# Splitting one sigmoid in two on ScalarE so that GpSimd's half of a gate comes first

**Chip, cores, metric.** One core of one Trainium2 chip. The time is device microseconds of one launch.

## The reference

```python
def _attn_ref(x):                       # x: (8, 3136, 256) fp32
    X = np.fft.fft(x, axis=1)
    X = np.fft.fft(X, axis=2)
    return X.real.astype(np.float32)

def _moe_ref(x, w_in, conv_w, w_out):   # d_ff = 1024, 3 taps
    h = np.maximum(x @ w_in, 0.0)
    # conv_out: depthwise convolution of h over the sequence, 3 taps
    gate = 1.0 / (1.0 + np.exp(-conv_out))
    return (h * gate @ w_out).astype(np.float32)
```

## The kernel before

The main loop has 256 steps: 8 batches, 4 chunks of positions, 8 slices of 128 rows of d_ff. A chunk is 769, 770, 770 or 833 columns wide. A step goes through these functions at different times; the loop is a software pipeline. In the same steps, side work prepares the next batch: VectorE folds x and builds w, TensorE does a part of the Fourier transform (`pd`), ScalarE copies half of its result (`as`), VectorE finishes it into `pt` and `qt`, and GpSimd treats one single row (`er`).

```python
    def combine(s):        # VectorE, one input in PSUM (a), one in SBUF (c): h
        ...
    def first_tap(s):      # ScalarE: g = h * cw[0]
        ...
    def other_taps(s):     # VectorE, h and g both in SBUF: "the taps", L504
        for k in (1, 2):
            stt(out=g, in0=h[:, k:k + n], scalar=cw[:, k, f:f + 1], in1=g, op0=ALU.mult, op1=ALU.add)

    def sigmoid(s):
        act(gs[s], gs[s], AF.Sigmoid)

    def gate(s):
        ...
        m = n // 2
        gt(g[:, m:n], g[:, m:n], h[:, m + 1:n + 1], op=ALU.mult)   # GpSimd, upper half
        vt(g[:, 0:m], g[:, 0:m], h[:, 1:m + 1], op=ALU.mult)       # VectorE, lower half

    # ---- where the side work of batch b is placed
        for i, u in enumerate(us):
            ...
            at(cs[i + 1], "act", u.copy)
            if i == 4:
                at(cs[i + 1], "dve", row)      # DMA er <- qt
            at(cs[i + 1], "dve", u.fin)        # for i == 4: GpSimd's work on er

    for t in range(n + LAG):
        ...
        if 0 <= t - 2 < n:
            sigmoid(steps[t - 2])
        if t + 1 < n:
            products(steps[t + 1])             # TensorE: pb, pa
            copies(steps[t + 1])               # ScalarE: nb <- pb, L481
        run("act")
        if t < n:
            combine(steps[t])
        run("load")
        run("dve")
        if t + 2 < n:
            seed(steps[t + 2])
        if t < n:
            first_tap(steps[t])
        if 0 <= t - 1 < n:
            other_taps(steps[t - 1])
        if 0 <= t - 2 < n:
            gate(steps[t - 2])
        if t >= LAG:
            mm2(steps[t - LAG])                # TensorE: po, needs both halves of g
        run("pe")
```

Each engine's list has this order, and its instructions in the timelines follow it: on ScalarE of the kernel before L507 starts at 631.33, L481 at 632.47, L309 at 633.23, L466 (`seed`) at 634.10 and L498 at 634.62.

## Time and profile before

| kernel before | |
|---|---|
| time, median of 4 runs | 1309.3 us (1307.4 to 1310.5) |
| span of the profiled run | 1303.7 us |
| TensorE / VectorE / ScalarE / GpSimd busy | 1203.4 / 1190.7 / 857.4 / 406.7 us |
| TensorE's wait for VectorE's half of the gate | 22.0 us in 43 waits |
| TensorE's wait for GpSimd's half of the gate | 14.9 us in 9 waits |

The busy shares cannot say which of two nearly full engines sets the time. The waits of TensorE for the gate can: they are the stretches in which VectorE or GpSimd is ahead of it in the chain. The prediction shows these lines.

### The profile page before, as it was taken

The numbers are of one execution on the slowest core, as the hardware profiler recorded it, in microseconds if no ns is written. First come the engines' busy times: TensorE is split into PE (matmuls) and PEld (weight loads), VectorE is DVE, ScalarE is ACT, GpSimd is POOL, SyncE is SP. The second block draws the span as 40 slices with busy tenths as digits, with TensorE's granted clock in tenths as the row PEclk, the third lists the DMA queues.
The fourth block names the chain that finished last, engine by engine and source line by source line (L and its number), as shares of the span: only waits on it lengthen the run. The fifth ranks groups of instructions, "written<-read, shape, count | busy, mean of one in ns | idle before, by whom it ended". The sixth has DMA issues, their size and how long they took to land.

```text
span 1303.7 us, 15202 instructions
## 1 busy us (share of the span) xinstructions
PE 1203.4 (92%) x4914; PEld 898.9 (69%) x4914; DVE 1190.7 (91%) x1664; ACT 857.4 (66%) x1558; POOL 406.7 (31%) x507
## 2 busy tenths in 40 slices
PE   0758999999999999999899999999999999999998
PEld 0525677777677766777677776777677777777776
DVE  6869999999999998999899998999989888898996
ACT  0226676666667666677667776766767777777885
POOL 2415434241523234232513225241322223122222
PEclk9968999999999999999999999999999999999999
DMA  7601203020211112020202103020010001000011
GB/s 227 185 25 45 80 25 99 1 77 25 88 36 49 49 29 74 25 77 25 72 29 62 39 25 94 30 76 1 25 50 25 27 25 42 20 14 27 25 33 43
DMA packets 46841, 66.02 MB, mean 51 GB/s; under 512 B 5601, under 2 KB 35197, under 8 KB 46505
## 3 DMA queue, kind: packets, MB, share of 16 engines
q1 hardware_dynamic: 41012, 49.80, 12.1%
q0 software_dynamic: 5120, 12.85, 3.4%
q10 hardware_dynamic: 628, 2.40, 0.6%
q8 instruction: 38, 0.62, 0.2%
q14 instruction: 43, 0.34, 0.1%
HBM read 39.24 MB, written 25.74 MB: 50 GB/s over the span
## 4 chain that ended last, share of the span: by engine, by line
PE 57%; DVE 26%; issue 8%; ACT 4%; POOL 2%; DMA 2%; DVEq 0%; POOLq 0%; ACTq 0%; SPq 0%
PE po L89 36%; PE pb L89 8%; DVE g L504 7%; PE pa L89 7%; PE pd L89 6%; DVE h L492 4%; DVE g L515 4%; ACT nb L481 2%; DVE w L174 2%; DVE w L175 1%; DVE xh L158 1%; DVE xh L147 1%; DVE xh L163 1%; POOL er L319 1%; DVE xh L162 1%
## 5 line engine op out<-in xcount | busy, mean ns | idle before, releaser
L89 PE MATMUL po<-wout,g 128*128 128x256 f32 (+2 forms) x3200 | 744.9, 383 | 37.4 <-DVE g L515 22.0
L89 PEld LDWEIGHTS po<-wout,g 128*128 128x128 f32 (+2 forms) x3200 | 598.6, 189 | 206.0 <-DVE g L515 59.2
L504 DVE SCALAR_TENSOR_TENSOR g<-h,cw,g 128x770 f32<-128x770 f32 (+2 forms) x512 | 579.9, 1133 | 10.9 <-ACT g L498 1.8
L514 POOL TENSOR_TENSOR g<-g,h 128x385 f32<-128x385 f32 (+1 forms) x256 | 240.5, 941 | 775.4 <-ACT g L507 434.7
L507 ACT ACTIVATE g<-g 128x770 f32<-128x770 f32 (+2 forms) x256 | 220.6, 862 | 253.3 <-DVE g L504 252.2
L481 ACT ACTIVATE nb<-pb 128x386 f32<-128x386 f32 (+4 forms) x512 | 225.8, 494 | 95.7 <-PE pb L89 94.0
L492 DVE CUSTOM_DVE_ANT_0 h<-pa,nb 128x386 f32<-128x386 f32 (+4 forms) x512 | 265.1, 559 | 14.6 <-PE pa L89 9.6
L498 ACT ACTIVATE g<-h,cw 128x770 f32<-128x770 f32 (+2 forms) x256 | 243.8, 952 | 0.7 <-DVE h L492 0.7
L89 PE MATMUL pa<-pt,G 128*128 128x386 f32 (+2 forms) x512 | 213.6, 498 | 9.1 <-ACT pa L466 9.1
L89 PE MATMUL pb<-qt,G 127*128 127x386 f32 (+2 forms) x512 | 215.7, 502 | 4.5 <-ACT nb L481 4.5
L466 ACT ACTIVATE pa<-eb,ge 128x386 f32<-128x386 f32 (+2 forms) x256 | 154.0, 602 | 8.1 <-DMA eb<-ed 8.1
L515 DVE TENSOR_TENSOR g<-g,h 128x385 f32<-128x385 f32 (+2 forms) x256 | 153.0, 598 | 4.2 <-ACT g L507 4.2
L89 PEld LDWEIGHTS pa<-pt,G 128*128 128x128 f32 x512 | 97.5, 191 | 83.6 <-issue 21.0
L89 PE MATMUL pd<-tab,w 99*128 99x196 f32 (+2 forms) x448 | 119.0, 375 | 0.0
L89 PEld LDWEIGHTS pb<-qt,G 127*128 127x128 f32 x512 | 94.3, 191 | 31.8 <-ACT nb L481 7.7
L122 POOL DMA_INDIRECT xh<-in_x_dram,idx x64 | 88.8, 1388 | 16.4 <-issue 12.8
L89 PEld LDWEIGHTS pd<-tab,w 99*128 99x128 f32 (+1 forms) x448 | 83.7, 191 | 13.7
L531 ACT COPY os<-po 128x256 f32<-128x256 f32 (+2 forms) x200 | 59.8, 393 | 17.1 <-DMA out_dram<-os 9.6
L158 DVE TENSOR_TENSOR xh<-xh 98x1024 f32<-98x1024 f32 (+1 forms) x32 | 46.6, 1460 | 0.1
L147 DVE TENSOR_TENSOR xh<-xh 98x1020 f32<-98x1020 f32 (+1 forms) x32 | 45.6, 1435 | 0.0
L89 PE MATMUL po<-win,dm 128*128 128x512 f32 x8 | 5.7, 879 | 38.4 <-DMA dm<-dft_dim_dram 38.4
L174 DVE TENSOR_TENSOR w<-xh 98x508 f32<-98x508 f32 (+1 forms) x32 | 31.1, 971 | 0.1
(84 smaller groups left out, 350.8 us busy)
## 6 DMA issues: line engine op xcount, KB each, us to landing
out_dram<-os SPq DMA_DIRECT2D x184, 128.0 KB
xh<-in_x_dram SPq DMA_DIRECT2D x16, 784.0 KB
eb<-ed SPq DMA_DIRECT2D x16, 193.0 KB
tab<-dft_seq_dram SPq DMA_DIRECT2D x4, 601.8 KB
raw<-in_moe_w_in_dram ACTq DMA_DIRECT2D x2, 1024.0 KB
raw<-in_moe_w_out_dram SPq DMA_DIRECT2D x1, 2048.0 KB
eb<-ed SPq DMA_DIRECT2D x8, 209.0 KB
eb<-ed SPq DMA_DIRECT2D x8, 192.5 KB
```

The source lines that it names most:

```text
L89: nc.tensor.matmul(o, l, r, start=start, stop=stop, skip_group_check=True)
L122: nc.gpsimd.indirect_dma_start(out=xh[b, h][0:NP, 4 + m].rearrange("p q d -> p (q d)"), out_offset=None, in_=bass.AP(tensor=x.tensor, offs ...
L158: vt(flat(to, to + 2), flat(0, 2), flat(2, 4), op=op)
L466: act(pa[s][:, 0:n], eb[b, c], AF.Copy, scale=ge[:, f:f + 1])
L481: act(nb[s][:, i, cols], p[:, cols], AF.Copy, scale=-1.0 if i else 1.0)
L492: nc.vector._custom_dve(TENSOR_ADD_SAT, out=to, in0=a[:, cols], in1=c[:, i, cols], s0=BIG, s1=0.0)
L498: act(gs[s], hs[s][:, 0:n], AF.Copy, scale=cw[:, 0, s[2]:s[2] + 1])
L504: stt(out=g, in0=h[:, k:k + n], scalar=cw[:, k, f:f + 1], in1=g, op0=ALU.mult, op1=ALU.add)
L507: act(gs[s], gs[s], AF.Sigmoid)
L514: gt(g[:, m:n], g[:, m:n], h[:, m + 1:n + 1], op=ALU.mult)
L515: vt(g[:, 0:m], g[:, 0:m], h[:, 1:m + 1], op=ALU.mult)
L531: nc.scalar.copy(out=osb[0:m, j % 2], in_=pt[0:m, j % 2])
```

## The change

GpSimd multiplies the upper half of the gate. With one sigmoid for the whole width it waits until the lower half is done too: 0.92 us from the sigmoid's start, 271.08 to 272.00 in the timeline that the prediction shows. The change does the upper half first, so that GpSimd starts earlier.

```diff
     def sigmoid(s):
-        act(gs[s], gs[s], AF.Sigmoid)
+
+        n = gs[s].shape[1]
+        for c in (slice(n // 2, n), slice(0, n // 2)):
+            act(gs[s][:, c], gs[s][:, c], AF.Sigmoid)
```

Line numbers after it shift by 3: GpSimd's half is L514 before and L517 after, VectorE's L515 and L518, the sigmoid L507 and L510.

## The prediction

> **What bounds the kernel now.** I read the page first (busy shares and groups), then the waits of TensorE, then the timeline of one steady batch step by step. "Step" is one pass of the main loop: one 128-row slice of F for one chunk of positions. There are 256, in 8 batches of 32.
>
> ```profile
> PE 1203.4 (92%) x4914; PEld 898.9 (69%) x4914; DVE 1190.7 (91%) x1664; ACT 857.4 (66%) x1558; POOL 406.7 (31%) x507
> ```
>
> TensorE and VectorE are both near full, ScalarE and GpSimd are not. The windows of the single batches say the same: batches 0 to 5 take 152 to 155 us with VectorE 143 to 148 us busy and TensorE 147 to 149; batch 6 takes 145 with TensorE busy 144; batch 7 takes 125 with TensorE busy 124. So the last two batches are TensorE's alone, and in the first six the two engines hand the lead to each other. The groups that matter:
>
> ```profile
> L504 DVE SCALAR_TENSOR_TENSOR g<-h,cw,g 128x770 f32<-128x770 f32 (+2 forms) x512 | 579.9, 1133 | 10.9 <-ACT g L498 1.8
> L514 POOL TENSOR_TENSOR g<-g,h 128x385 f32<-128x385 f32 (+1 forms) x256 | 240.5, 941 | 775.4 <-ACT g L507 434.7
> L507 ACT ACTIVATE g<-g 128x770 f32<-128x770 f32 (+2 forms) x256 | 220.6, 862 | 253.3 <-DVE g L504 252.2
> L515 DVE TENSOR_TENSOR g<-g,h 128x385 f32<-128x385 f32 (+2 forms) x256 | 153.0, 598 | 4.2 <-ACT g L507 4.2
> ```
>
> GpSimd's 775 us of idle is its own and costs nothing by itself; what matters is when its multiply (L514) runs. The timeline of two steps of batch 1 shows that:
>
> ```profile
> 271.08 0.85 ACT L507 ACTIVATE g<-g 128x769 f32<-128x769 f32 x1 [2.02 <-DVE g L504]
> 271.43 1.02 DVE L492 CUSTOM_DVE_ANT_0 h<-pa,nb 128x385 f32<-128x385 f32 x2
> 271.56 2.86 PE L89 MATMUL po<-wout,g 128*128 128x256 f32 x12 [0.72 <-DVE g L515]
> 272.00 0.86 POOL L514 TENSOR_TENSOR g<-g,h 128x385 f32<-128x385 f32 x1 [4.05 <-DVE h L492]
> 272.36 2.38 DVE L504 SCALAR_TENSOR_TENSOR g<-h,cw,g 128x769 f32<-128x769 f32 x2
> ...
> 274.77 0.85 ACT L507 ACTIVATE g<-g 128x769 f32<-128x769 f32 x1 [0.76 <-DVE g L504]
> 275.12 1.02 DVE L492 CUSTOM_DVE_ANT_0 h<-pa,nb 128x385 f32<-128x385 f32 x2
> 275.69 0.86 POOL L514 TENSOR_TENSOR g<-g,h 128x385 f32<-128x385 f32 x1 [1.80 <-DVE h L492]
> 276.05 1.05 DVE L174 TENSOR_TENSOR w<-xh 99x508 f32<-99x508 f32 x1
> 277.02 0.68 DVE L175 TENSOR_TENSOR w<-xh 99x508 f32<-99x508 f32 x1
> 277.62 2.07 DVE L504 SCALAR_TENSOR_TENSOR g<-h,cw,g 128x769 f32<-128x769 f32 x2
> ...
> 280.21 2.86 PE L89 MATMUL po<-wout,g 128*128 128x256 f32 x12 [0.59 <-DVE g L515]
> ```
>
> The sigmoid starts when VectorE's taps (L504) end; 0.92 us later GpSimd starts its 0.86 us multiply. VectorE is meanwhile in the combine (L492, one input in PSUM), which runs at its usual 1.02 us for two. The instruction after the combine has two SBUF inputs, and it is stretched for as long as GpSimd still runs: the taps take 2.38 us in the first step and 2.07 in the second, where GpSimd is done before they start; there L174 takes 1.05 us instead of about 0.68. The stretch is GpSimd's end (272.86) less the combine's (about 272.45): 0.3 to 0.4 us. Steps with 833 columns show 0.39 to 0.42. Taking each form's tenth-percentile duration in the trace as undisturbed, the stretch sums to about 55 us on L504, 10 on L515 and 29 on the folding operations: some 94 us of VectorE's busy time.
>
> [...]
>
> **The change part by part.** Nothing moves between engines, and no queue is reordered; ScalarE's list gains 256 instructions.
> 1. *ScalarE.* 256 sigmoids of 862 ns become 512 of half the width. [...] ScalarE has 102 to 106 us busy in a batch of 152 to 155, so this mostly fills idle time.
> 2. *GpSimd.* The half that it multiplies comes first, so its start moves from 0.92 us after the sigmoid's start to about 0.60, an estimate: 0.32 us earlier (0.35 with 833 columns). The duration is as before.
> 3. *VectorE.* GpSimd now ends about 0.05 us after the combine instead of 0.37. Each stretched pair loses about 0.32 us. GpSimd's new start is still after L515, so it does not collide there. I find about 150 steps of 256 where GpSimd starts straight after the sigmoid and an operation with two SBUF inputs follows, so L504 should lose some 35 to 45 us of its 580 and the folds about 12.
> 4. *What of it reaches the end.* Only where TensorE waits for VectorE. Those waits are few:
>
> ```profile
> PE po L89 <- DVE g L515: 22.0, 43, 1.9
> PE po L89 <- POOL g L514: 14.9, 9, 2.9
> ```
>
> By batch the first is 8.7, 4.0, 3.0, 2.3, 2.0, 2.0, 0 and 0 us. The gap in the issue of matmuls is some 0.16 us larger each time, so about 29 us, the upper limit. But not all these waits come from a stretched chain. Many follow a step like this one:
>
> ```profile
> 314.20 0.52 DVE L258 TENSOR_TENSOR qt<-as,pd 128x197 f32<-128x197 f32 x1 [1.33 <-ACT as L254]
> ...
> 316.06 2.06 DVE L504 SCALAR_TENSOR_TENSOR g<-h,cw,g 128x770 f32<-128x770 f32 x2
> ...
> 318.64 2.86 PE L89 MATMUL po<-wout,g 128*128 128x256 f32 x12 [0.36 <-DVE g L515]
> ```
>
> VectorE first waited 1.33 us for TensorE's transform (pd, through ScalarE), then ran unstretched (2.06 us, GpSimd was long done), and TensorE waited for the result. Nothing in that loop gets shorter. I went through the waits one by one and allowed each only the stretch that lies between VectorE's last idle time (or the previous wait) and it, 0.32 us a step and never more than the gap. Batch 0: steps 1 to 10, each with a fold, run without a break, 10 x 0.32 = 3.2 us, and two later waits 0.7: 4. Batch 1: 2.6. Batch 2: 1.0. Batches 3, 4 and 5: three waits each of about 0.33, 0.29 and 0.5, so 1.1 each. Batches 6 and 7: nothing. The sum is about 11 us.
> 5. *Taken back.* In a few steps the copies behind the sigmoid (L481, then the transform's copy L254) start the moment it ends, and VectorE waits for them; there 0.1 us is lost, some two steps a batch, under 2 us in all.
>
> 1308.8 - 11 + 1.5 = **1299 us**, 0.7% faster.
>
> **The rivals.**
> *The saving on VectorE goes all the way.* If VectorE paced the first six batches throughout, about 0.32 us x 20 steps x 6 = 38 us would come off: 1270 us, 3% faster. For it: VectorE hardly pauses in most steps, and the chain of the page gives it 26%. Against it: TensorE's own matmuls issue in about 144.6 us a batch, so that most of the 153 us is already TensorE, and after a saving VectorE would only wait longer for pd.
> *ScalarE becomes the bound or delays the chain.* It would lose 0.1 to 0.2 us a step where its copies release VectorE: up to 0.15 x 200 = 30 us, 1335. For it: L481 follows the sigmoid in order, and L254 follows L481. Against it: ScalarE waits 94 us in all for TensorE's pb just before L481, and 252 us for L504 before the sigmoid; both swallow the extra.
> *GpSimd is late for another reason.* Nine waits on its multiply (14.9 us) stand behind the single-row work on er (L317 to L319, up to 2.4 us each) and not behind the sigmoid; likewise where its indirect transfers are in the way. Then the earlier half changes nothing: if this held more widely, the time stays at 1305 to 1309.
>
> **Range and chances.** The step accounting can err by half on either side: 4 to 17 us saved, and a little more if shorter VectorE steps let TensorE run ahead over several steps; on the other side the full ScalarE cost. I take 1288 to 1308. Two per cent faster would need 26 us, almost all the waits, 5%; two per cent slower needs a new bound, 2%.
>
> **What the profile after would show.** Right: a sigmoid half of 0.51 to 0.55 us; GpSimd's multiply starting about 0.6 us after the first half's start; L504's mean down from 1133 to about 1050 ns; VectorE's busy time down 40 to 60 us while the span falls far less; TensorE's wait for VectorE's gate down from 22 us to 12 to 15, left mostly behind transform steps; VectorE's waits for as (L254, L273) longer. Wrong: L504 unchanged (then GpSimd doesn't start earlier, or collides elsewhere); VectorE's gate waiting for the second half; L481 waiting no longer for pb; or the span falling by as much as VectorE's busy time.

## The result, and the profile after

1289.3 us, median of 4 runs (1287.4 to 1290.5): a ratio of 0.9847, 95% interval 0.9829 to 0.9865, or 20 us off. A ratio here is the mean time of one kernel's fast runs over that of the other's of the same rounds, so not quite the ratio of the medians quoted. The predicted 1299 us had half of this gain; the time lies 1.3 us inside the lower end of the predicted range.

The page of the changed kernel, busy shares and groups:

```profile
PE 1198.0 (93%) x4914; PEld 898.6 (70%) x4914; DVE 1153.2 (90%) x1664; ACT 880.2 (68%) x1814; POOL 404.1 (31%) x507
L504 DVE SCALAR_TENSOR_TENSOR g<-h,cw,g 128x770 f32<-128x770 f32 (+2 forms) x512 | 556.9, 1088 | 11.0 <-ACT g L498 1.5
L510 ACT ACTIVATE g<-g 128x385 f32<-128x385 f32 (+3 forms) x512 | 244.1, 527 | 187.6 <-DVE g L504 187.3
```

VectorE is 37.5 us less busy. The taps' mean fell from 1133 to 1088 ns. A half sigmoid takes 527 ns.

The timeline of the changed kernel at the two steps that the prediction showed:

```profile
269.25 0.94 ACT L510 ACTIVATE g<-g 128x385 f32<-128x385 f32 x2 [1.46 <-DVE g L504]
269.60 1.02 DVE L492 CUSTOM_DVE_ANT_0 h<-pa,nb 128x385 f32<-128x385 f32 x2
269.74 2.86 PE L89 MATMUL po<-wout,g 128*128 128x256 f32 x12 [0.22 <-DVE g L518]
269.86 0.86 POOL L517 TENSOR_TENSOR g<-g,h 128x385 f32<-128x385 f32 x1 [3.13 <-ACT g L510]
270.53 2.07 DVE L504 SCALAR_TENSOR_TENSOR g<-h,cw,g 128x769 f32<-128x769 f32 x2
...
273.92 0.72 DVE L174 TENSOR_TENSOR w<-xh 99x508 f32<-99x508 f32 x1
```

GpSimd starts 0.61 us after the sigmoid's start (0.92 before). The taps take 2.07 us (2.38 before) and L174 0.72 us (1.05 before). TensorE's wait at the start of the first step has gone from 0.72 to 0.22 us.

The waits of TensorE after:

```profile
PE po L89 <- DVE g L518: 13.7, 27, 1.6
PE po L89 <- POOL g L517: 12.7, 10, 2.1
```

To see where the time came from I took every pair of successive matmuls in both traces and subtracted the first one's own time at full clock (the median distance of starts for its shape, 215 ns for 128x256 and 326 ns for 128x386) from the distance of their starts. What is left is a gap. Summed over the steps of a batch:

| batch | 0 | 1 | 2 | 3 | 4 | 5 | 6 | 7 | all |
|---|---|---|---|---|---|---|---|---|---|
| gaps before, us | 17.6 | 9.6 | 9.9 | 8.4 | 9.2 | 8.5 | 2.1 | 1.4 | |
| gaps after, us | 13.7 | 6.7 | 7.6 | 6.0 | 6.0 | 4.7 | 2.1 | 1.5 | |
| less by | 3.9 | 2.9 | 2.3 | 2.4 | 3.2 | 3.8 | 0 | -0.1 | 18.4 |
| predicted | 4 | 2.6 | 1.0 | 1.1 | 1.1 | 1.1 | 0 | 0 | 11 |

Batches 0 and 1 came as predicted. Batches 2 to 5 gave 11.7 us where 4.3 were predicted. Step by step, 5.0 of these 11.7 us lie at the waits for GpSimd's gate that stand behind its work on `er`. The prediction had said that nothing changes there. The other 6.7 us lie at waits for VectorE.

### The profile page after: what moved, and what is told of

It is laid out like the page before. It is cut to its first block, busy times and chain, and to the rows that moved or that the text cites. A ratio compares the mean times of both kernels' runs of the same rounds, so it can differ in the third digit from the quotient of the medians.

```text
span 1288.0 us, 15443 instructions
## 1 busy us (share of the span) xinstructions
PE 1198.0 (93%) x4914; PEld 898.6 (70%) x4914; DVE 1153.2 (90%) x1664; ACT 880.2 (68%) x1814; POOL 404.1 (31%) x507
## 4 chain that ended last, share of the span: by engine, by line
PE 69%; DVE 17%; issue 4%; ACT 4%; DMA 3%; POOL 2%; DVEq 0%; SPq 0%; ACTq 0%; POOLq 0%
PE po L89 43%; PE pb L89 10%; PE pa L89 9%; PE pd L89 7%; DVE g L504 4%; DVE h L492 2%; DVE g L518 2%; ACT nb L481 2%; DMA dm<-dft_dim_dram 1%; POOL er L319 1%; DVE w L174 1%; DVE xh L147 1%; DVE w L175 1%; DVE xh L158 1%; ACT g L510 1%
## 5 line engine op out<-in xcount | busy, mean ns | idle before, releaser
L89 PE MATMUL po<-wout,g 128*128 128x256 f32 (+2 forms) x3200 | 740.1, 381 | 26.6 <-DVE g L518 13.7
L504 DVE SCALAR_TENSOR_TENSOR g<-h,cw,g 128x770 f32<-128x770 f32 (+2 forms) x512 | 556.9, 1088 | 11.0 <-ACT g L498 1.5
L517 POOL TENSOR_TENSOR g<-g,h 128x385 f32<-128x385 f32 (+1 forms) x256 | 239.5, 937 | 755.2 <-ACT g L510 571.7
L510 ACT ACTIVATE g<-g 128x385 f32<-128x385 f32 (+3 forms) x512 | 244.1, 527 | 187.6 <-DVE g L504 187.3
L481 ACT ACTIVATE nb<-pb 128x386 f32<-128x386 f32 (+4 forms) x512 | 225.5, 494 | 121.8 <-PE pb L89 120.9
L518 DVE TENSOR_TENSOR g<-g,h 128x385 f32<-128x385 f32 (+2 forms) x256 | 155.2, 606 | 5.3 <-ACT g L510 5.3
L122 POOL DMA_INDIRECT xh<-in_x_dram,idx x64 | 88.0, 1374 | 16.4 <-issue 13.7
L147 DVE TENSOR_TENSOR xh<-xh 98x1020 f32<-98x1020 f32 (+1 forms) x32 | 43.0, 1353 | 0.0
L158 DVE TENSOR_TENSOR xh<-xh 98x1024 f32<-98x1024 f32 (+1 forms) x32 | 41.2, 1294 | 0.1
```

What stands on the lines that cost most here:

```text
L89: nc.tensor.matmul(o, l, r, start=start, stop=stop, skip_group_check=True)
L122: nc.gpsimd.indirect_dma_start(out=xh[b, h][0:NP, 4 + m].rearrange("p q d -> p (q d)"), out_offset=None, in_=bass.AP(tensor=x.tensor, offs ...
L147: vt(a[:, :, :, 1:D], a[:, :, :, 1:D], r[:, :, :, D - 1:0:-1], op=ALU.add)
L481: act(nb[s][:, i, cols], p[:, cols], AF.Copy, scale=-1.0 if i else 1.0)
L510: act(gs[s][:, c], gs[s][:, c], AF.Sigmoid)
```

## The experiments

Three questions: is it really GpSimd's position in time that makes VectorE faster; what does ScalarE's extra work cost; and why did the waits behind the work on `er` get shorter? Then two attempts at the waits that are left. Experiments 1 to 4 ran on one chip in one call, 5, 6, 9 and 10 in a second, 7, 8, 11 and 12 in a third. Across calls I compare ratios to the kernel before.

### 1. The order of the halves swapped

```diff
-        for c in (slice(n // 2, n), slice(0, n // 2)):
+        for c in (slice(0, n // 2), slice(n // 2, n)):
```

> The change with the order of its halves swapped: VectorE's half of the sigmoid first, GpSimd's second. Theory (the gain is GpSimd's earlier end[...]): GpSimd's multiply starts about 1.0 us after the sigmoid's start (0.92 before, 0.65 in the change), the taps L504 rise from 1133 ns of the kernel before to about 1150 to 1165, and the time is 1309 to 1316 us. Rival (splitting the sigmoid gains by itself, whatever the order, for instance because the queue of ScalarE is rearranged): time near 1289.

Measured: 1314.1 us, ratio to the kernel before 1.0032 (1.0015 to 1.0049). The groups and TensorE's waits of this run:

```profile
L504 DVE SCALAR_TENSOR_TENSOR g<-h,cw,g 128x770 f32<-128x770 f32 (+2 forms) x512 | 588.4, 1149 | 10.7 <-ACT g L498 1.6
PE po L89 <- DVE g L518: 27.0, 48, 2.0
```

The same two instructions in the other order make the kernel slower than before, by 5 us. GpSimd starts 1.02 us after the sigmoid's start (584.14 to 585.16 in the timeline). The taps are stretched more, 1149 ns, and TensorE waits longer for VectorE, 27.0 us. So the split gains nothing by itself. The order, and with it GpSimd's place in time, is what counts: three positions of GpSimd (0.61, 0.92 and 1.02 us) give the taps 1088, 1133 and 1149 ns.

### 2. GpSimd's multiply replaced by a fill that reads nothing

Based on the kernel before; the result is wrong on purpose.

```diff
-        gt(g[:, m:n], g[:, m:n], h[:, m + 1:n + 1], op=ALU.mult)
+        nc.gpsimd.iota(g[:, m:n], pattern=[[1, n - m]], base=0, channel_multiplier=1, ...)
```

> The kernel before with one sigmoid, and GpSimd's multiply replaced by a fill of the same half with an iota, which reads no SBUF tensor; the result is wrong on purpose. Theory[...]: GpSimd still starts 0.9 us after the sigmoid's start and still overlaps the taps, but L504 is near its undisturbed 1020 to 1040 ns. Rival (any GpSimd instruction that writes there at that time slows VectorE): L504 stays stretched in proportion to the overlap. If the fill takes a very different time than 0.87 us, the overlap has to be compared, not the means. Time, if L504 is undisturbed: 1285 to 1293 us.

Measured: 1284.7 us, ratio 0.9813. The taps' mean was 1038 ns. But the fill takes 0.46 us and not 0.87 (458 ns, the mean of its group of 192). It is mostly over before the taps start, so the mean says little, as was foreseen. The overlaps have to be compared. In this run 13 taps overlapped the fill by 0.35 to 0.5 us, and none was stretched by more than 0.01 us. In the kernel before, 102 taps overlapped the multiply by 0.48 to 0.70 us (mean 0.58) and were stretched by 0.36 us on average. But this pair is not alike: 12 of the 13 taps began before the fill, and the taps of the kernel before that began before the multiply (6, overlapped by 0.49 to 0.66 us) were not stretched either, at most by 0.014 us. There it was the multiply that got longer. So the like cases are those in which GpSimd starts while a tap runs. First the multiply of the kernel before, then the fill:

```profile
264.00 1.27 POOL L514 TENSOR_TENSOR g<-g,h 128x385 f32<-128x385 f32 x1 [4.88 <-ACT g L507]
262.80 0.46 POOL L514 IOTA g<- 128x385 f32 x1 [1.94 <-DVE w L175]
```

In the kernel before, 15 multiplies began with 0.43 to 0.91 us of the running tap left and took 1.21 to 1.68 us instead of 0.87 or 0.92. Here 11 fills began with 0.44 to 1.00 us left and took 0.46 to 0.50 us, as all fills do. In the two steps shown the pair of taps took 2.55 us with the multiply (the second one was stretched) and 2.07 us with the fill. So in these cases the fill and the taps did not lengthen each other; the multiply and the taps did, and the one that started later (by 0.1 us or more in these cases) took longer. Whether it is the reads, or something else in which a fill differs from a multiply, was not shown. The lengthening was less than the overlap: the taps lost 0.36 us at a mean overlap of 0.58 us, and between 0.01 and 0.05 us at mean overlaps of 0.18 and 0.24 us (75 taps of the changed kernel); the multiply at 264.00 lost 0.40 us with 0.55 us of the tap left. A part of the taps' is that records overlap: in the timelines shown, the taps' begins 0.09 us before the combine's ends. What the rest is, was not tested. The run also gives the size of the prize: with nearly all the stretch gone, the span loses 21 us, against 16 with the change. GpSimd's shorter time is in this number too.

### 3. One more cut of the lower half

```diff
-        for c in (slice(n // 2, n), slice(0, n // 2)):
+        for c in (slice(n // 2, n), slice(n // 4, n // 2), slice(0, n // 4)):
```

> The change with VectorE's half of the sigmoid cut once more into two quarters, GpSimd's half still first: GpSimd starts as in the change, ScalarE does 256 more instructions, about 0.1 us more occupancy a step. Theory (ScalarE's cost is hidden but for a few steps): L504 stays at 1088 ns and the time is 1289 to 1292 us. Rival (ScalarE's extra work is a real part of the chain, and ate part of the gain): 1295 us or more.

Measured: 1290.6 us, ratio 0.9851 (0.9834 to 0.9867), against 0.9847 for the change. The taps are at 1086 ns as there. Another 256 instructions on ScalarE cost about 1 us, which these rounds do not resolve. ScalarE's work is hidden, as predicted.

### 4. The lower half behind the copies

```diff
         if 0 <= t - 2 < n:
-            sigmoid(steps[t - 2])
+            sigmoid(steps[t - 2], False)       # upper half
         if t + 1 < n:
             products(steps[t + 1])
             copies(steps[t + 1])
         run("act")
+        if 0 <= t - 2 < n:
+            sigmoid(steps[t - 2], True)        # lower half
```

> The change with VectorE's half of the sigmoid moved behind the copies L481 of the same step on ScalarE (and behind the transform's copies), GpSimd's half still first. Theory (in transform steps where ScalarE's copies follow the sigmoid at once, the chain runs from VectorE through ScalarE back to VectorE, and the split lengthens it by about 0.1 us): these steps get about 0.4 us shorter where the copies do not wait for pb, and the time falls by 1 to 5 us against the change, to 1284 to 1288. Rival (the copies always wait for TensorE's pb): 1288 to 1291, no difference.

Measured: 1287.9 us, ratio 0.9834 (0.9817 to 0.9850). That is 1.4 us under the change, with overlapping intervals: inconclusive. If ScalarE's longer sigmoid cost anything, it is about this much. Its copies L481 wait 159.4 us for pb here, against 120.9 in the change, so most of what they could gain is swallowed by that wait.

### 5 and 6. The work on er behind the gate

GpSimd's list has the work on `er` (L317 to L319) ahead of the gate of the same step. The gate is ready first, but it waits in line: in batch 3 of the kernel before its sigmoid ended at 632.18, the row work started at 634.69 and the gate behind it at 640.38.

```diff
-            at(cs[i + 1], "dve", u.fin)
+            at(cs[i + 1], "pool" if i == 4 else "dve", u.fin)
 ...
             gate(steps[t - 2])
+        run("pool")
```

On the kernel before:

> The kernel before with the single-row work on er (GpSimd, L317 to L319, and its DMA out) issued behind the gate of the same step instead of ahead of it. GpSimd then no longer holds a ready gate back for the row's inputs. Theory: TensorE's waits for GpSimd's gate (14.9 us in 9) nearly vanish, 10 to 18 us off, 1291 to 1299 us. Rival (the gate of the next step then waits behind the 5.8 us of row work just as long): no gain, 1305 to 1311.

On the change:

> The change, with the row work on er behind the gate as in er_late_before. Theory for what the prediction missed (about 5 us of the change's gain came through the load queue: L175 on VectorE, then the queue's load of x, then the row of er, then GpSimd's row work, then a gate that TensorE waits for): with that wait removed in both kernels the change is worth only 12 to 16 us, so 1276 to 1285 us and a ratio to er_late_before of 0.988 to 0.991. Rival (the whole extra gain is from steps whose VectorE chain I counted too strictly): the change is worth its full 18 to 21 us here too.

Measured: 1298.5 us (ratio to the kernel before 0.9919) and 1278.1 us (0.9767). The move gains about 10 us on either kernel. The change over its own base is 0.9767 / 0.9919 = 0.9847: its full worth, 20 us, and not the 12 to 16 that I expected. As a test of the `er` path it failed, though, and the trace tells why: the waits had not gone as expected. Three of the nine were left, 6.8 us on the kernel before and 3.8 us on the change. In batch 3 the gap at this place is 2.45 us with the kernel before as base, followed by 1.67 us that matmuls at half rate cost (see 7 and 8), and 1.52 and 0 us with the change. So the change still saves time there. The link had to be cut elsewhere.

### 7 and 8. The row's transfer ahead of the load

This is the path, in the timeline of the kernel before, batch 3:

```profile
628.63 0.68 DVE L175 TENSOR_TENSOR w<-xh 98x508 f32<-98x508 f32 x1
629.37 0.36 SPq L111 DMA_DIRECT2D xh<-in_x_dram  x1
629.78 0.70 SPq L328 DMA_DIRECT2D er<-qt  x1
634.69 0.88 POOL L317 TENSOR_TENSOR er<-as 1x197 f32<-1x197 f32 x1 [6.52 <-ACT pa L466]
637.85 2.63 POOL L319 TENSOR_SCALAR er<-er 1x392 f32<-1x392 f32 x1
640.38 0.86 POOL L514 TENSOR_TENSOR g<-g,h 128x385 f32<-128x385 f32 x1
641.29 1.56 PE L89 MATMUL po<-wout,g 128*128 128x256 f32 x6 [2.68 <-POOL g L514]
```

The load of x (L111) waits in the sync queue for the fold L175 on VectorE, which frees its buffer: it is issued 0.06 us after L175 ends. The row's transfer (L328) stands behind it in the same queue. The trace's semaphore waits have it landing at 634.58. GpSimd starts its row work 0.1 us later, then does the gate, and TensorE waits for that. So a faster fold on VectorE pulls this whole chain forward. In the change (same view, same place) the row work starts right at the end of ScalarE's copy L309:

```profile
621.01 0.67 DVE L175 TENSOR_TENSOR w<-xh 98x508 f32<-98x508 f32 x1
622.15 0.70 SPq L328 DMA_DIRECT2D er<-qt  x1
626.24 0.96 ACT L309 COPY as<-pd 1x394 f32<-1x394 f32 x2
627.20 0.74 POOL L317 TENSOR_TENSOR er<-as 1x197 f32<-1x197 f32 x1 [6.66 <-ACT as L309]
```

The experiment cuts the link: the row is sent some two steps earlier, ahead of the load.

```diff
-            if i == 4:
-                at(cs[i + 1], "dve", row)
+            if i == 3:
+                at(cs[i + 1] + 1, "act", row)
```

> The kernel before with the row's transfer (er from qt, L328) put ahead of the load of x (L111) in the sync queue, so that it no longer stands behind the load's wait for VectorE's L175. In er_late the wait had not gone, so this cuts the link itself. Theory: the row lands several us before it is needed, GpSimd's row work starts at the end of ScalarE's L309 and no longer some 0.4 to 0.5 us after it, and TensorE's wait for GpSimd's gate falls by about 0.4 us in batches 2 to 4: 1306 to 1309 us, 0 to 3 us off. Rival (the link does not matter): the row work starts as late as before.

> The change with the row's transfer ahead of the load. In the change the row already landed (627.09) before L309 ended (627.20), so there is little left: 1287 to 1290 us. Theory: the waits for GpSimd's gate in batches 2 to 4 differ from row_early_before by clearly less than the 0.6 us of the pair before/after, about 0.1 to 0.2, and the change is worth 16 to 19 us here. Rival: the difference of these waits stays 0.6, and the worth 20 us.

Measured: on the kernel before 1303.5 us, ratio 0.9958 (0.9943 to 0.9973); on the change 1288.7 us, ratio 0.9847 (0.9832 to 0.9862), no different from the change alone. With the link cut, the change is worth 0.9847 / 0.9958 = 0.989, that is 14.8 us instead of 20. In batches 2 and 3, the gaps behind the row work now differ by only 0.25 and 0.21 us between the two kernels; between before and after they differ by 0.62 and 0.65. So in these two batches about two thirds of the gain at this place came through the sync queue. It is not so in the others. In batch 1 the difference grew from 0.08 to 0.82 us, in 4 and 5 it hardly moved, and over all batches these waits (without the half-rate stretches below) gain 2.1 us from the change with the link cut and 2.2 us without. The expected difference of 0.1 to 0.2 us and worth of 16 to 19 us were both missed a little.

The gain on the kernel before was larger than the 0 to 3 us that I expected. A second thing explains part of it. Two of these waits in the kernel before were followed by slow matmuls. TensorE's timeline and two windows of the kernel before:

```profile
793.98 2.93 PE L89 MATMUL po<-wout,g 128*128 128x256 f32 x6 [2.95 <-POOL g L514]
794.50:796.50 2.00, 2.00 (x6) 1.57 (x5) 2.00 (x4) 0.00 (x0) 1.70 (x2) 0.50 0.25 71
639.90:646.00 6.10, 4.50 (x18) 3.28 (x18) 4.70 (x6) 2.13 (x5) 5.57 (x5) 1.00 0.12 37
```

The first line has the six matmuls that took 1.56 us at 641.29, now in 2.93 us. In the window lines the third number from the end is the granted clock: 0.50 there, 1.00 around the other wait. So half rate followed the wait of 2.95 us and one of 1.93 us (946.80 to 949.00, clock 0.55), but not the one of 2.68 us: the length of a single wait does not tell. What does was not shown. Taking half of the time that TensorE was occupied at the clock of 0.50 as lost, such stretches after the loop's first steps (from 110 us on) cost 4.8 us in the profiled run of the kernel before: 1.7 us in batch 0, and 3.1 us behind the row work in batches 4 and 5. With the row sent early it is 1.7 us, in the change nothing. Of the some 3.4 us by which the gaps of the second pair differ less than those of the first, these 3.1 us are nearly all. So the fall of the change's worth from 20 to 14.8 us does not measure the link.

### 9. The transform's copies first

After the change most of TensorE's waits for VectorE are in steps with transform work. There VectorE waits for the copies `as`, and these stand behind the copies L481 on ScalarE, which wait for pb. The copies only need pd, which is done earlier: the 56 copies of the changed kernel start 1.4 to 2.2 us after the last matmul of their pd ends.

```diff
+        run("act")
         if t + 1 < n:
             products(steps[t + 1])
             copies(steps[t + 1])
-        run("act")
```

> The change, with the transform's copies (L254, L273, L309) put ahead of the copies L481 on ScalarE, so that they start when the transform's matmuls (pd) end and not after pb and two copies. Theory (after the change TensorE's waits for VectorE that are left stand behind transform steps in which VectorE waits for these copies): VectorE's waits for as fall by half or more from 78 us, TensorE's waits for its gate from 13.7 to under 9 us, time 1277 to 1286. Rival (VectorE then only waits elsewhere, TensorE being the bound): 1287 to 1291.

Measured: 1269.2 us, ratio to the kernel before 0.9696 (0.9673 to 0.9720). It beat its range. VectorE's waits for `as` fell from some 76 to 38 us, and TensorE's wait for its gate from 13.7 to 6.0. Most of the waits for GpSimd's gate stay, 8.8 of 12.7 us.

### 10, 11 and 12. Together

> The change with both: row work behind the gate, and the transform's copies first. If both waits are separate the gains add up: 1265 to 1277 us. If TensorE's issue (about 144.6 us a batch in batches 1 to 5) is then the only bound, nothing below about 1258 us is possible.

This is the change with the edits of 5 and 9. Measured: 1259.4 us, ratio 0.9624 (0.9599 to 0.9649), the fastest of all, again under its range and near the 1258 us that were called the floor. TensorE's waits for the gate are 5.4 us for VectorE and 1.7 for GpSimd.

> The kernel before with the transform's copies first and the row work behind the gate, without the split sigmoid: is the split still worth something once TensorE waits for little else? as_er_after took 1259 us. Theory (TensorE waits wherever VectorE's chain is unbroken, and with early copies it is unbroken for longer, so more of the stretch counts): 1280 to 1292 us, the split worth 20 to 33 us. Rival (TensorE is then the bound, the stretch is hidden): 1262 to 1270.

The same two edits without the split sigmoid. Measured: 1269.4 us, ratio 0.9695 (0.9679 to 0.9711). I was wrong about this one: the split is worth about 10 us here (0.9624 / 0.9695), not 20 to 33. The taps are still stretched (1146 ns, against 1104 in as_er_after), but TensorE's wait for VectorE is only 8.8 us. With the copies early, TensorE is the bound nearly everywhere, and most of VectorE's stretch is hidden.

> The best guess: the change, VectorE's half of the sigmoid behind the copies L481, the transform's copies first, the row work behind the gate, and the row's transfer ahead of the load. as_er_after has 7 us left of TensorE's waits for VectorE and GpSimd, mostly in batch 0. 1254 to 1259 us; if TensorE is the bound, no better than as_er_after (1259).

The change with the edits of 4, 5, 7 and 9. Measured: 1262.3 us, ratio 0.9640 (0.9626 to 0.9654). The 1254 to 1259 us were missed. It is no better than as_er_after, as was foreseen if TensorE is the bound; whether it is really worse was not measured in the same rounds.

## Why the prediction was right or wrong

**The bound.** Right: VectorE and TensorE take turns, and only the waits of TensorE count. VectorE lost 37.5 us of busy time, the span 15.7 and the time 20. Batches 6 and 7, TensorE's own, gained nothing.

**Step 1, ScalarE.** Right in size: 527 ns for a half (0.51 to 0.55 expected), two in 0.94 us. The total grew by 23 us, from 857.4 to 880.2. The two halves overlap by about 0.11 us (2 x 527 ns, and 0.94 us for the two), and the page has 244.1 us for L510, less than 512 x 527 ns, some 270 us.

**Step 2, GpSimd's start.** Right: 0.61 us after the sigmoid's start (0.60 estimated), so 0.31 us earlier. The 0.32 us in the prediction was my estimate; no trace of the kernel before has a sigmoid of half the width.

**Step 3, VectorE.** The direction was right, and swapping the order confirmed it: the earlier GpSimd starts, the shorter the taps (1088, 1133 and 1149 ns at 0.61, 0.92 and 1.02 us). Why an overlapping multiply lengthens them was not shown. VectorE lost 37.5 us, just under the 40 to 60 that were expected. The size was off for the taps: they lost 23 us, where 35 to 45 were expected, and stand at 1088 and not 1050 ns; the folds lost 17, where 12 were expected, and VectorE's half of the gate took 2.2 us more, where no collision was expected. I had counted steps in which TensorE leads. There the sigmoid starts later against VectorE, and even the earlier multiply still lies on the taps: by the same measure VectorE's whole stretch in batch 7 went from 15.2 to 15.6 us. Nothing hangs on it, since VectorE is not the bound there.

**Step 4, what reaches the end.** This is the term that was mis-sized: 11 us predicted, 18.4 us of gaps measured. Batches 0 and 1 fit (6.6 and 6.8), batch 0 in part by luck: its half-rate stretch, 1.7 us, is in the kernel before alone, and two waits of 0.68 us behind it in the change alone. In batches 2 to 5 two assumptions failed.
- The prediction named as a rival that nine waits stand behind the work on `er` "and not behind the sigmoid", so that the earlier half changes nothing there. They gave 5.0 us in these batches. 3.1 us of it are the two half-rate stretches behind them, which nothing in the prediction foresaw; the waits themselves got 1.9 us shorter. In batches 2 and 3, 0.37 and 0.44 us of that came from VectorE's fold through the sync queue, as cutting the link showed. Where the rest came from stays open.
- I gave no credit to waits behind a transform step, because VectorE "first waited for TensorE's transform". In some of those steps it waited for ScalarE alone. Step 122 of the kernel before shows it:

```profile
690.44 0.90 ACT L507 ACTIVATE g<-g 128x833 f32<-128x833 f32 x1 [1.77 <-DVE g L504]
691.25 0.91 ACT L481 ACTIVATE nb<-pb 128x418 f32<-128x418 f32 x2
692.04 0.32 ACT L254 COPY as<-pd 128x196 f32<-128x196 f32 x1
692.40 0.52 DVE L258 TENSOR_TENSOR pt<-as,pd 128x196 f32<-128x196 f32 x1 [0.49 <-ACT as L254]
```

The copies follow the sigmoid without a wait for pb, and the sigmoid starts when VectorE's taps end. The chain goes from VectorE through ScalarE back to VectorE, so an earlier end of VectorE counts. The gap after this step went from 0.29 us to nothing (its like in batches 2, 4 and 5: 0.14 to 0.38 us). That is 1.1 of the remaining 2.4 us. Part of the rest lies at the first wait of each of these batches, which lost 0.55 to 0.61 us, where no wait of batches 3 to 5 had been allowed more than about 0.5. It was not followed further.

**Step 5, taken back.** About right: one such step grew by 0.09 us; over the whole kernel it is 1 us or so, at the limit of what the runs resolve.

**The rivals.** "The saving goes all the way" (38 us) was wrong, since TensorE's own time, about 144.6 us of a batch, stays; the fill of experiment 2 removed nearly all the stretch and gained only 25 us. "ScalarE becomes the bound" was wrong (experiment 3); its sum was too, 1308.8 + 30 is 1339 and not 1335. "GpSimd is late for another reason" was right that these waits stand behind the row work, and wrong that the change does nothing to them.

What stays open: how much of the measured 20 us is due to the half-rate stretches. In the profiled pair it is 4.8 us, of which three waits of 0.68 us that the change alone has behind such places took back 2.0. What decides whether a wait is followed by half rate was not shown (2.95 and 1.93 us were, 2.68 us was not), and only one run of each kernel was profiled. The profiled run of the kernel before, 1305.4 us, was faster than all but one of its other runs, so that the two spans differ by 15.7 us only. Part of that is seen: TensorE started on the second step at 90.2 us there and at 92.7 us in the change, before any code that the edit touches has run.

## What to carry to other kernels

When one engine's instruction lengthens another's that it overlaps (here the taps by 0.36 us at an overlap of 0.58 us), the first is worth moving in time even off the critical path: find what it overlaps, and let it overlap work that it does not disturb (here the combine, 1.02 us for two as before). To say what such a saving is worth, follow each wait of the bounding engine back to its true start, through DMA queues and in-order neighbours too; an engine's idle time does not end the chain if what ended it came from the same engine. And when a ready instruction stands in line behind one that waits (the copies behind L481, the gate behind `er`), moving it ahead can be worth more than any change of durations: here 20 us and about 10 us for two edits.
